# One load's issue and one cast trade places in GpSimd's order, in a fused attention and adapter kernel

## The chip, the core and the metric

The kernel runs on one core of a Trainium2 chip. The core has a matrix engine (TensorE, PE in the profile; its weight loads are PEld), a vector engine (VectorE, DVE), an activation engine (ScalarE, ACT), GpSimd (POOL) and a small engine that here only issues transfers (SyncE, SP). Data moves between the memory outside (DRAM) and the core's on-chip memory by 16 DMA engines, which serve several queues. The metric is the time of one execution on the device in microseconds (us); less is better.

## The reference

Two stages. The first is attention over 8 batch rows, 8 heads, 576 positions and head size 64, with a window of 32 positions: the plain last 32 for heads 0 to 3, and every fourth of the last 128 for heads 4 to 7. The second is a mixture of 8 low-rank adapters (rank 16), of which each token takes the best two:

```python
    mask_plain = (rel >= 0) & (rel < window)
    mask_dil = (rel >= 0) & (rel < window * dilation) & (rel % dilation == 0)
    ...
    scores = np.where(masks[None, :, :, :], scores, -1000000000.0)
    attn = np.exp(scores - max); attn = attn / sum
    x = np.matmul(attn, v)                       # [8*576, 512]
    ...
    logits = x @ w_gate                          # 8 experts, the best two by softmax
    delta[mask] += w[mask, k, None] * (x[mask] @ A[e] @ B[e])
    return x + delta
```

(The lines are condensed from the reference; inputs are float32, random with a fixed seed.)

## The kernel before

The work is cut by batch row r (0 to 7) and head group g (0: the plain heads, 1: the dilated heads, whose positions are sorted so that they too become a plain band). Each piece of work is an operation with a short name, an engine, the names that it depends on, and, if it uses PSUM, a bank. A text, PLAN, lists all 427 names in one order; the program emits them in that order, each to its own engine. So for every engine the order of its work is the order of its names in PLAN, and between engines only the waits on semaphores count, which are worked out from the dependencies. An operation whose dependencies its engine has already waited for, directly or through others, gets no wait.

The names, with row r and group g:

- L2 to L6 load a row's queries, keys and values into one of four input slots (row r into slot r mod 4), as two transfers each, one for each half of 64 partitions. Row 7 alone is loaded in eight smaller transfers: Lq7gh brings queries and keys of group g for the half h of the partitions (288 KB each in the profile), Lv7gh the values (146.2 KB each). All of these are issued by GpSimd, by `nc.gpsimd.dma_start` in line 272 (line 275 for L2 to L6).
- S0rg and S1rg are the scores on TensorE, E0rg and E1rg the exponentials on ScalarE, Vrg the product with the values on TensorE, Rrg and Nrg the reciprocal and the normalisation on VectorE (lines 381 and 384), which write the row's result X in float32.
- Brg is the cast of X to bf16 on GpSimd (line 391), Trg and Ur the transposes of it on TensorE, Crg, Cdr, Cpr their copies on ScalarE.
- Z, Y, m, s12, tt, th, top, g2 work out the logits and the gates; gzr (line 493) multiplies them on GpSimd; G transposes, gc and gn copy, D multiplies with B, and A adds the result to X (on VectorE; A73, A53, A63 in line 553 and A42, A52, A62, A72 in line 573 on GpSimd).
- Or (and Org for the last two rows) are the stores, issued by SP. Each waits for its row's A operations and, by the list `late`, for the four Lq transfers of row 7 and for Lv710 and Lv711. Each whole-row store also waits for the store before the last one to have landed.

Row 7's loads go into slot 3, which row 3 used; all eight depend on the same list, the scores and value products of row 3:

```python
        elif r == B - 1:
            free = used[r - SLOTS]
            for g in range(2):
                qk_ready[r, g] = [load(f"Lq{r}{g}{h}", r, [(h, QK_AT[h][g], QK)], free) for h in range(2)]
                v_ready[r, g] = [load(f"Lv{r}{g}{h}", r, [(h, V_AT[h][g], VB)], free) for h in range(2)]
                late.extend(qk_ready[r, g] + v_ready[r, g] * g)
```

B50, the cast of row 5's first half, depends on N50 and on the last readers of the cast's buffer, T30 and U3:

```python
        free = [f"T{r - 2}{g}", f"U{r - 2}"] if r > 1 else []
        add(f"B{tag}", "POOL", ("el", cut), lambda: [nc.gpsimd.tensor_copy(XB[r % 2][:, g, 0:cut], X[r][:, XG * g : XG * g + cut])], [nm] + free)
```

GpSimd's order around the change is, before: B40, Lq700, Lq701, B41, Lq710, gz3, B50, Lq711, Lv710, Lv711, B51, Lv700, Lv701, B60, gz4. TensorE's order in the same stretch is S150, V51, T40, T41, V50, D22, U4, G3, D21, Z04, S060, D32, Z14, S161, S160, T50, D30, S061, V60, T51, V61, U5, S171, S070, Z05, Z15, S170, S071.

Of the kernel before, what the change touches and what calls it, by code (L numbers as in the profile page):

```python
# [593 lines left out]


PLAN = """
pz0 wz warm@4 F1@1 awf btf vz00 pz2 con vz10 Lk00 Lk01 Lv00 Lv01
S000@6 vz01 vz11 tab cc1 cd3 vz20 cc0 vz21 cd2 cd0 L11 pz1 E000
F2@1 L10 cd1 S100@4 S101@6 E100 E101 L2 S001@2 E001 V00@4 R00 N00 V01@1
L3 R01 F0@0 xz0 B00 N01 B01 T00@4 vz30 L4 pz3 C00 S111@5 E111  # L600
awc S011@2 U0@0 T01@7 E011 V11@3 Cd0 Cp0 S010@1 C01 R11 vz31 E010 N11
Z00@0 Y00 m00 Z10@6 Y10 m10 S110@4 B11 s120 E110 tt0 th0 top0 V10@2
g20 gz0 T11@5 R10 N10 btc G0@1 gc0 D01@6 B10 gn0 D00@0 C11 xz1
U1@4 Cd1 Cp1 T10@5 C10 A01 A00 S121@6 E121 S120@3 S021@1 Z01@0 E021 Z11@5
Y01 m01 Y11 m11 L5 s121 S020@1 D02@0 V21@5 E120 top1 tt1 th1 g21
E020 A02 V20@0 R21 N21 R20 gz1 G1@5 gn1 F3@6 S130@6 N20 gc1 B21 E130
S031@3 D12@2 E031 S030@0 D10@5 T21@7 E030 C21 A12 S131@3 B20 V30@0 A10 E131
U2@7 T20@6 R30 N30 Cp2 B30 L6 V31@3 Cd2 C20 Z02@7 Y02 Z12@1 R31
N31 B31 T30@2 D11@6 Y12 C30 S041@4 A11 E041 S141@2 S140@6 m02 E141 S040@0
m12 s122 tt2 U3@5 Cp3 th2 E040 top2 Cd3 g22 gz2 V41@2 T31@0 E140  # L610
C31 V40@5 R41 N41 Z03@2 G2@0 Y03 gn2 Z13@1 gc2 R40 Y13 N40 B40
S051@2 D20@4 E051 A20 m13 S151@6 E151 Lq700 S050@0 S150@2 E150 m03 s123 V51@5
top3 tt3 T40@3 th3 Lq701 E050 C40 B41 g23 T41@4 C41 R51 Lq710 V50@0
N51 R50 D22@5 N50 U4@7 gz3 Cd4 Cp4 G3@6 gn3 D21@3 gc3 A22 A21
Z04@7 Y04 B50 Lq711 S060@0 D32@2 Z14@7 S161@5 m04 E060 Y14 m14 E161 s124
S160@0 A32 Lv710 T50@7 E160 D30@3 S061@5 top4 V60@0 A30 tt4 R60 C50 Lv711
O1 E061 B51 T51@3 N60 C51 V61@4 th4 g24 R61 N61 U5@7 S171@2 Cp5
Cd5 S070@0 Z05@7 E171 E070 Z15@6 Y05 S170@2 S071@4 Y15 Lv700 m05 m15 top5
Lv701 B60 gz4 E170 E071 s125 G4@0 B61 D31@6 tt5 th5 gn4 V70@1 T60@4
A31 gc4 V71@5 U6@0 C60 O0 g25 O2 gz5 G5@4 Cp6 Cd6 R70 N70  # L620
B70 T61@2 D41@0 D42@3 R71 N71 gn5 A41 C61 dx4 gc5 B71 Bx7 D40@5
Z06@2 Y06 Z16@4 Y16 A40 m06 A42 D52@3 m16 s126 dx5 top6 U7@7 Cp7
Cd7 tt6 T71@1 Cx7 C71 T70@4 D51@5 A52 th6 g26 A51 D50@0 A50 C70
gz6 Z07@2 Z17 m07 m17 s127 tt7 dy5 G6@5 gc6 O3 D61@0 th7 gn6
D62@7 A53 top7 O4 dx6 g27 D60@5 gy7 gz7 A62 dy6 O5 A61 A63
O61 G7@3 H7 gm7 gn7 gc7 D72@0 dx7 A72 D71@1 A60 D73@6 O60 A71
D70@7 O71 A70 dy7 A73 O70
"""

_INS = ["qkv", "aw", "bt", "con"]  # L630
# [60 lines left out]
```

## Time and profile before

| | us |
|---|---|
| median of 3 runs | 101.55 |
| lowest and highest of the runs | 101.32, 101.83 |
| the profiled execution's own time | 101.17 |
| its span in the profile | 99.4 |

| engine | busy us, share of the span |
|---|---|
| TensorE (matmuls) | 81.2, 82% |
| ScalarE | 71.0, 71% |
| VectorE | 62.0, 62% |
| GpSimd | 51.6, 52% |

The profile shows one execution. Times in it are counted from the start of the span. A row of the timeline gives start, duration, engine, line, operation, output and input, and in brackets how long the engine was idle before it and which engine ended that wait; "issue" is put there where the profile shows nothing that was waited for. A table of stretches gives, for each stretch of the span, the busy time and the number of instructions of each engine, then TensorE's granted clock, the share of time in which the DMA engines were busy, and what they moved in GB/s. In the queues' view q0 are the loads that GpSimd issues, q1 the stores of SP, and q8 the engines' instructions; a row gives packets, MB and the time that the packets took as a share of 16 engines' time. Landings are given as time from issue until the data has arrived.

### The profile page before, as it was taken

The page shows a single profiled execution, that of the slowest core. Times are in us where ns is not written, and L with a number is a line of the kernel's source. Part 1 is how long each engine was busy: PE and PEld are TensorE (multiplying, and loading weights), DVE is VectorE, ACT ScalarE, POOL GpSimd, SP SyncE. Part 2 cuts the span into 40 slices and gives each one's busy share as a digit, 9 for nine tenths or more (in the row PEclk, how much of TensorE's full clock was granted, in tenths as well). Part 3 has the DMA queues.
Part 4 walks back from the last instruction along what each step waited for, and adds up shares of the span by engine and source line. Part 5 has one row for each costly group of instructions (what it writes and reads, how often), then busy time and mean ns, then how long its engine had stood idle before and what let it go on. Part 6 is the DMA issues. An engine that isn't in the chain of part 4 may idle for free.

```text
span 99.4 us, 3604 instructions
## 1 busy us (share of the span) xinstructions
PE 81.2 (82%) x1587; PEld 59.8 (60%) x1587; DVE 62.0 (62%) x138; ACT 71.0 (71%) x123; POOL 51.6 (52%) x68
## 2 busy tenths in 40 slices
PE   3999969869568988999995968999999999777500
PEld 2443557458445864889674847877888878564300
DVE  5770008606469188259736665796895999979810
ACT  5294592499858964796895695979989989957400
POOL 5999402851548054404922095449458365574820
PEclk9999999999999999999999999999999999999955
DMA  1999999999999999999999999997999999839994
GB/s 19 318 206 207 207 216 228 209 209 214 207 211 217 218 216 208 209 214 205 216 208 214 218 210 210 219 197 122 198 326 408 415 412 412 352 163 415 386 421 202
DMA packets 5727, 24.50 MB, mean 247 GB/s; under 512 B 720, under 2 KB 848, under 8 KB 4944
## 3 DMA queue, kind: packets, MB, share of 16 engines
q0 software_dynamic: 3840, 14.23, 72.5%
q1 hardware_dynamic: 1728, 9.77, 24.1%
q8 instruction: 12, 0.20, 0.8%
q10 hardware_dynamic: 144, 0.28, 0.7%
q14 instruction: 3, 0.02, 0.1%
HBM read 29.07 MB, written 9.44 MB: 387 GB/s over the span
## 4 chain that ended last, share of the span: by engine, by line
PE 43%; DMA 28%; DVE 9%; ACT 6%; POOL 4%; issue 4%; POOLq 0%
PE ps L212 39%; DMA in<-in_qkv_dram 28%; DVE x L384 4%; PE ps L408 3%; ACT p L345 2%; DVE x L545 2%; POOL xb L391 2%; POOL x L553 1%; PE ps L498 1%; ACT gn L517 1%; ACT xt L418 1%; DVE rec L381 1%; POOL x L573 1%; DVE top L486 1%; ACT gc L514 1%
## 5 line engine op out<-in xcount | busy, mean ns | idle before, releaser
L391 POOL CAST xb<-x 128x1152 bf16<-128x1152 f32 (+1 forms) x16 | 18.2, 1140 | 27.6 <-DVE x L384 27.6
L345 ACT ACTIVATE p<-ps 128x960 bf16<-128x960 f32 (+1 forms) x32 | 27.6, 899 | 5.5 <-PE ps L212 5.4
L212 PE MATMUL ps<-in,p 128*64 128x130 bf16 (+1 forms) x416 | 21.3, 221 | 3.3 <-ACT p L345 3.1
L384 DVE TENSOR_TENSOR x<-ps,rec 128x1152 f32<-128x1152 f32 x16 | 21.7, 1357 | 0.5
L212 PEld LDWEIGHTS ps<-in,p 128*64 128x64 bf16 (+1 forms) x416 | 17.1, 104 | 6.7 <-ACT p L345 4.4
L545 DVE TENSOR_TENSOR x<-x,ps 128x1024 f32<-128x1024 f32 (+1 forms) x16 | 17.5, 1115 | 3.4 <-PE ps L212 3.4
L381 DVE RECIPROCAL rec<-ps 128x18 f32<-128x18 f32 x16 | 4.3, 270 | 17.4 <-PE ps L212 17.2
L493 POOL TENSOR_TENSOR gz<-zs,g 128x640 bf16<-128x640 f32 x7 | 8.9, 1275 | 11.1 <-DVE g L488 11.1
L212 PE MATMUL ps<-warm 128*128 128x512 f32 x22 | 12.7, 720 | 1.5 <-DVE warm L216 1.5
L212 PE MATMUL ps<-in 64*64 64x96 bf16 (+1 forms) x576 | 11.9, 201 | 1.5 <-issue 1.5
L212 PEld LDWEIGHTS ps<-in 64*64 64x64 bf16 x576 | 10.9, 106 | 3.7 <-issue 1.8
L272 POOL DMA_DIRECT2D in<-in_qkv_dram x22 | 11.7, 587 | 0.8 <-POOLq L674 0.8
L212 PE MATMUL ps<-aw,xt 128*128 128x136 bf16 x160 | 11.3, 223 | 0.1
L408 PE MATMUL ps<-one,xb 128*128 128x128 bf16 x128 | 9.6, 219 | 1.2 <-issue 1.2
L418 ACT COPY xt<-ps 128x1024 bf16<-128x1024 bf16 x8 | 8.1, 1011 | 3.4 <-PE ps L408 3.3
L212 PEld LDWEIGHTS ps<-aw,xt 128*128 128x128 bf16 x160 | 9.6, 98 | 0.9 <-ACT xt L418 0.4
L408 PEld LDWEIGHTS ps<-one,xb 128*128 128x128 bf16 x128 | 7.6, 97 | 2.5 <-issue 1.3
L212 PEld LDWEIGHTS ps<-warm 128*128 128x128 f32 x22 | 4.7, 232 | 6.3 <-issue 4.8
L421 ACT COPY xt<-ps 128x1024 bf16<-128x1024 bf16 x7 | 7.2, 1034 | 1.4 <-PE ps L408 1.4
L212 PE MATMUL ps<-bt,gn 128*128 128x256 bf16 (+1 forms) x48 | 6.8, 263 | 1.5 <-ACT gn L517 0.8
L212 PE MATMUL ps<-bt,gc 128*128 128x256 bf16 (+1 forms) x48 | 6.6, 255 | 1.5 <-ACT gc L514 1.5
L466 ACT COPY zs<-ps 128x408 f32<-128x408 f32 (+1 forms) x14 | 5.9, 459 | 2.0 <-PE ps L212 2.0
(54 smaller groups left out, 98.0 us busy)
## 6 DMA issues: line engine op xcount, KB each, us to landing
in<-in_qkv_dram POOLq DMA_DIRECT2D x10, 868.5 KB, 23.1
out_dram<-x SPq DMA_DIRECT2D x6, 1152.0 KB, 5.8
in<-in_qkv_dram POOLq DMA_DIRECT2D x10, 288.0 KB, 8.1
out_dram<-x SPq DMA_DIRECT2D x4, 576.0 KB, 3.0
in<-in_qkv_dram POOLq DMA_DIRECT2D x10, 146.2 KB, 8.1
in<-in_qkv_dram POOLq DMA_DIRECT2D x2, 434.2 KB, 13.5
awf<-in_aw_dram ACTq DMA_DIRECT2D x1, 272.0 KB, 3.7
btf<-in_bt_dram SPq DMA_DIRECT2D x1, 256.0 KB, 3.5
```

The lines of the kernel that those rows point to most:

```text
L212: return nc.tensor.matmul(o, lhsT=lhsT, rhs=rhs, start=start, stop=stop, skip_group_check=True)
L272: nc.gpsimd.dma_start(out=IN[r % SLOTS][half(a), at : at + n], in_=qkv[r, a, :, at - 2 * VB * a : at - 2 * VB * a + n],) if n < ROW else n ...
L345: return [nc.scalar.activation(p[:, :, :].rearrange("p h (s c) -> p h s c", c=PER)[:, :, b0 : b0 + nb, 0:SEG], PS[:, k.at : k.at + 2, 0 : ...
L381: rc = add(f"R{tag}", "DVE", ("el", 60), lambda: [nc.vector.reciprocal(rec[:, :].rearrange("p (b i) -> p b i", b=3), PS[:, k.at : k.at + 3 ...
L384: nm = add(f"N{tag}", "DVE", ("el", XG), lambda: [nc.vector.tensor_tensor(X[r][:, XG * g : XG * g + XG].rearrange("p (b i n) -> p b i n", ...
L391: add(f"B{tag}", "POOL", ("el", cut), lambda: [nc.gpsimd.tensor_copy(XB[r % 2][:, g, 0:cut], X[r][:, XG * g : XG * g + cut])], [nm] + free)
L408: nc.tensor.transpose(tp[j][:, 128 * u : 128 * u + 128], xb[:, g, 256 * u + 128 * j : 256 * u + 128 * j + 128], ident())
L418: return [nc.scalar.copy(xt[:, 0:2, 0:S].rearrange("p j (c i) -> p j c i", c=C)[:, :, :, 0:128], tp.rearrange("p j (i c) -> p j c i", c=C))]
L421: return [nc.scalar.copy(xt[:, 2:4, 0:512], tp)]
L466: zc.append(add(f"Y{st}{r}", "ACT", ("el", len(us) * ZW), lambda us=us, k=k: [nc.scalar.copy(zs[:, us[0] : us[-1] + 1].rearrange("p u n -> ...
L493: return [en.tensor_tensor(GZ[i][:, us[0] : us[0] + n, :].rearrange("p u (e r) -> p u e r", e=E), zv()[:, us[0] : us[0] + n, 0:ER].rearran ...
L545: return [nc.vector.tensor_tensor(v, v, PS[:, k.at : k.at + nk].rearrange("p b n -> p (b n)"), ALU.add)]
```

## The change

In PLAN, and so in GpSimd's order, Lq711 now stands ahead of B50 where it stood right behind it. All other names keep their places; the text of PLAN is only broken into lines afresh. The order on the other engines stays the same, and no operation is added or taken away. The diff cut to its core:

```diff
 ...
-Z04@7 Y04 B50 Lq711 S060@0 D32@2 Z14@7 S161@5 m04 E060 Y14 m14 E161 s124
+gn3 D21@3 gc3 A22 A21 Z04@7 Y04 Lq711 B50 S060@0 D32@2 Z14@7 S161@5 m04
 ...
```

GpSimd's order afterwards is: B40, Lq700, Lq701, B41, Lq710, gz3, Lq711, B50, Lv710, Lv711, B51, Lv700, Lv701, B60, gz4.

More of the change, by code (lines that the diff above doesn't have):

```diff
@@ L596 @@
 PLAN = """
[L597 to L612, printed above, removed]
@@ L613 @@
-top3 tt3 T40@3 th3 Lq701 E050 C40 B41 g23 T41@4 C41 R51 Lq710 V50@0
-N51 R50 D22@5 N50 U4@7 gz3 Cd4 Cp4 G3@6 gn3 D21@3 gc3 A22 A21
-Z04@7 Y04 B50 Lq711 S060@0 D32@2 Z14@7 S161@5 m04 E060 Y14 m14 E161 s124
[L616 to L627, printed above, removed]
+pz0 wz warm@4 F1@1 awf btf vz00 pz2 con vz10 Lk00 Lk01 Lv00 Lv01 S000@6
+vz01 vz11 tab cc1 cd3 vz20 cc0 vz21 cd2 cd0 L11 pz1 E000 F2@1 L10 cd1
@@ new lines @@
+S100@4 S101@6 E100 E101 L2 S001@2 E001 V00@4 R00 N00 V01@1 L3 R01 F0@0
+xz0 B00 N01 B01 T00@4 vz30 L4 pz3 C00 S111@5 E111 awc S011@2 U0@0 T01@7
+E011 V11@3 Cd0 Cp0 S010@1 C01 R11 vz31 E010 N11 Z00@0 Y00 m00 Z10@6 Y10
+m10 S110@4 B11 s120 E110 tt0 th0 top0 V10@2 g20 gz0 T11@5 R10 N10 btc
+G0@1 gc0 D01@6 B10 gn0 D00@0 C11 xz1 U1@4 Cd1 Cp1 T10@5 C10 A01 A00
+S121@6 E121 S120@3 S021@1 Z01@0 E021 Z11@5 Y01 m01 Y11 m11 L5 s121
+S020@1 D02@0 V21@5 E120 top1 tt1 th1 g21 E020 A02 V20@0 R21 N21 R20 gz1
+G1@5 gn1 F3@6 S130@6 N20 gc1 B21 E130 S031@3 D12@2 E031 S030@0 D10@5
@@ new lines @@
+T21@7 E030 C21 A12 S131@3 B20 V30@0 A10 E131 U2@7 T20@6 R30 N30 Cp2 B30
+L6 V31@3 Cd2 C20 Z02@7 Y02 Z12@1 R31 N31 B31 T30@2 D11@6 Y12 C30 S041@4
+A11 E041 S141@2 S140@6 m02 E141 S040@0 m12 s122 tt2 U3@5 Cp3 th2 E040
+top2 Cd3 g22 gz2 V41@2 T31@0 E140 C31 V40@5 R41 N41 Z03@2 G2@0 Y03 gn2
+Z13@1 gc2 R40 Y13 N40 B40 S051@2 D20@4 E051 A20 m13 S151@6 E151 Lq700
+S050@0 S150@2 E150 m03 s123 V51@5 top3 tt3 T40@3 th3 Lq701 E050 C40 B41
+g23 T41@4 C41 R51 Lq710 V50@0 N51 R50 D22@5 N50 U4@7 gz3 Cd4 Cp4 G3@6
@@ new lines @@
+gn3 D21@3 gc3 A22 A21 Z04@7 Y04 Lq711 B50 S060@0 D32@2 Z14@7 S161@5 m04
+E060 Y14 m14 E161 s124 S160@0 A32 Lv710 T50@7 E160 D30@3 S061@5 top4
+V60@0 A30 tt4 R60 C50 Lv711 O1 E061 B51 T51@3 N60 C51 V61@4 th4 g24 R61
+N61 U5@7 S171@2 Cp5 Cd5 S070@0 Z05@7 E171 E070 Z15@6 Y05 S170@2 S071@4
+Y15 Lv700 m05 m15 top5 Lv701 B60 gz4 E170 E071 s125 G4@0 B61 D31@6 tt5
+th5 gn4 V70@1 T60@4 A31 gc4 V71@5 U6@0 C60 O0 g25 O2 gz5 G5@4 Cp6 Cd6
+R70 N70 B70 T61@2 D41@0 D42@3 R71 N71 gn5 A41 C61 dx4 gc5 B71 Bx7 D40@5
@@ L628 @@
+Z06@2 Y06 Z16@4 Y16 A40 m06 A42 D52@3 m16 s126 dx5 top6 U7@7 Cp7 Cd7 tt6
+T71@1 Cx7 C71 T70@4 D51@5 A52 th6 g26 A51 D50@0 A50 C70 gz6 Z07@2 Z17
+m07 m17 s127 tt7 dy5 G6@5 gc6 O3 D61@0 th7 gn6 D62@7 A53 top7 O4 dx6 g27
+D60@5 gy7 gz7 A62 dy6 O5 A61 A63 O61 G7@3 H7 gm7 gn7 gc7 D72@0 dx7 A72
+D71@1 A60 D73@6 O60 A71 D70@7 O71 A70 dy7 A73 O70
 """
```

## The prediction

> **What bounds the kernel now.** I read the page's engine lines and its chain first, then the stretches of the chain on the timeline.
>
> ```profile
> PE 81.2 (82%) x1587; PEld 59.8 (60%) x1587; DVE 62.0 (62%) x138; ACT 71.0 (71%) x123; POOL 51.6 (52%) x68
> PE 43%; DMA 28%; DVE 9%; ACT 6%; POOL 4%; issue 4%; POOLq 0%
> q8 instruction: 12, 0.20, 0.8%
> in<-in_qkv_dram POOLq DMA_DIRECT2D x10, 288.0 KB, 8.1
> 20.58 27.80 DMA in<-in_qkv_dram
> ...
> 78.97 1.29 PE ps L212 x26
> ```
>
> The chain of waits is led by TensorE. In order of time (the last two rows) it is the load queue until 48.4 us and TensorE from about there to 80.26 us, where V71 ends, so the edited stretch (63 to 70 us) lies where TensorE sets the pace, and GpSimd is half idle. The third line is a queue that no line of the kernel issues: 12 transfers, 0.20 MB, 16 KB each. They are the program's own instructions. The fourth has the size of row 7's Lq transfers.
>
> The second view is GpSimd's timeline around the edit.
>
> ```profile
> 60.40 0.53 POOL L272 DMA_DIRECT2D in<-in_qkv_dram  x1
> 62.05 1.27 POOL L493 TENSOR_TENSOR gz<-zs,g 128x640 bf16<-128x640 f32 x1 [1.11 <-DVE g L488]
> 65.86 1.14 POOL L391 CAST xb<-x 128x1152 bf16<-128x1152 f32 x1 [2.55 <-DVE x L384]
> 66.95 1.62 POOL L272 DMA_DIRECT2D in<-in_qkv_dram  x3
> 68.52 1.20 POOL L391 CAST xb<-x 128x1152 bf16<-128x1152 f32 x1
> 69.61 1.07 POOL L272 DMA_DIRECT2D in<-in_qkv_dram  x2
> ```
>
> These are Lq710, gz3, B50, then Lq711 with Lv710 and Lv711, B51, then Lv700 with Lv701. GpSimd stands idle for 2.55 us ahead of B50, waiting for VectorE's N50; the moved issue sat behind that wait and now goes in front of it.
>
> The third view is TensorE's weight loads where they stopped for no reason on another engine, and with it the table of stretches cut at these stops.
>
> ```profile
> 53.61 0.32 PEld L408 LDWEIGHTS ps<-one,xb 128*128 128x128 bf16 x5 [1.30 <-issue]
> 60.12 0.11 PEld L212 LDWEIGHTS ps<-in 64*64 64x64 bf16 x2 [1.43 <-issue]
> 66.63 0.22 PEld L212 LDWEIGHTS ps<-in 64*64 64x64 bf16 x14 [0.34 <-issue]
> core 0: us, PE busy (x) PEld busy (x) DVE busy (x) ACT busy (x) POOL busy (x), PEclk, DMA share, GB/s
> 53.60:60.10 6.50, 5.21 (x127) 4.19 (x126) 4.02 (x11) 4.46 (x7) 2.97 (x4) 1.00 1.06 213
> 60.10:66.60 6.50, 6.27 (x126) 5.31 (x127) 4.82 (x9) 5.53 (x10) 2.84 (x4) 1.00 1.05 213
> 66.60:71.20 4.60, 4.58 (x128) 3.69 (x128) 3.48 (x11) 4.07 (x6) 4.07 (x7) 1.00 0.87 151
> 71.20:75.94 4.74, 4.72 (x128) 4.01 (x129) 3.33 (x5) 4.07 (x9) 2.75 (x3) 1.00 1.06 330
> ```
>
> Three stops, two of them in the middle of one score tile, and between one and the next 126 to 127 pairs of weight load and matmul: about 254 instructions, a 16 KB block. I read them as TensorE having run out of instructions. By the same count the next two blocks begin at 71.20 and at 75.94, and there it did not stop.
>
> The fourth view, the queues in narrow stretches, says when a block was fetched. These are 57.45 to 57.50, 64.00 to 64.05, 67.7 to 67.8 and 72.98 to 73.05 (the share is of 16 engines in the stretch, so 160.0% of 0.05 us is 1.28 us for the transfer).
>
> ```profile
> q8 instruction: 1, 0.02, 160.0%
> q8 instruction: 1, 0.02, 156.1%
> q8 instruction: 1, 0.02, 55.9%
> q8 instruction: 1, 0.02, 115.4%
> ```
>
> Durations: 1.28, 1.25, 0.89 and 1.29 us. The first two end at 58.75 and 65.27, and TensorE goes on at 60.12 and 66.63: 1.37 us later, both times. And if a block is asked for when the one before it begins, the transfer started 3.86 us after the asking (53.61 to 57.47) and 3.90 us (60.12 to 64.02) with the load queue full, but 1.12 us (66.63 to 67.75) in the third stretch. That stretch is the one with 151 instead of 213 GB/s. The hole, 62 GB/s over 4.60 us or 0.285 MB, is nearly one Lq transfer (288.0 KB, 0.295 MB): the one that the edit brings forward.
>
> **The change part by part.** The cast and the issue trade places in GpSimd's order; nothing is added or removed. Lq711 has no wait of its own left (Lq700 waited for the same list), so it can go when gz3 ends, at 62.05 + 1.27 = 63.32, and its 0.53 us (Lq710's row) end at 63.85, 2.0 us before B50 can start. B50 therefore loses nothing: cover 2.55, cost 0.53; were the idle time gone, B50 would be 0.53 us late. Behind B50 the two remaining issues end 0.53 us earlier, and B51 starts at 67.99 instead of 68.52. TensorE does not use that:
>
> ```profile
> 68.56 0.45 PEld L408 LDWEIGHTS ps<-one,xb 128*128 128x128 bf16 x8
> 71.21 0.49 PEld L408 LDWEIGHTS ps<-one,xb 128*128 128x128 bf16 x8
> 73.24 0.14 PEld L212 LDWEIGHTS ps<-con,one 64*64 64x64 bf16 x4 [0.16 <-issue]
> ```
>
> T51 reads B51 at 71.21, 1.5 us after the cast ended. So on GpSimd the change is worth zero.
>
> On the load queue, the landings of Lq710, Lq711 and the last pair of late loads, from the loads' view in the stretches 60 to 61, 66.9 to 67.4 and 67.9 to 68.5:
>
> ```profile
> DMA to landing us min/median/max: 8.3/8.3/8.3
> DMA to landing us min/median/max: 4.0/4.0/4.0
> DMA to landing us min/median/max: 4.1/4.2/4.3
> ```
>
> Lq710 lands at 68.7, Lq711 at 70.95, and Lv711, the third of three issues that take 1.62 us from 66.95 on, at 68.03 + 4.3 = 72.3. Issued at 63.3, Lq711 follows Lq710 directly: 0.295 MB at 213 GB/s is 1.38 us, so it lands at about 70.1, 0.85 us earlier. Its first reader S171 starts at 73.24 (the row above), so that is worth zero as well; the late loads are done 0.5 to 0.8 us earlier, which only lets the stores begin.
>
> What is left is what the filled hole does to the instruction block that TensorE needs at 71.20. No run shows a fetch behind exactly this queue, so I bound its lag. Lower end: 1.12 us as now. Upper end: 3.9 us, the full queue of the earlier stretches. To do no harm it must start by 71.20 - 1.37 - 1.28 = 68.55, a lag of 1.92. In my reading the fetch waits for the descriptors that already stand on its engine; before, those were the rest of Lq710, afterwards that rest and Lq711: 1.12 + 1.38 = 2.50 us. I take this value, since it is made of the nearest row and of the one transfer that moves. The fetch then starts at 69.13, takes 1.28 (the load queue is full again, Lv710 being there from 66.95 on), and TensorE goes on at 69.13 + 1.28 + 1.37 = 71.78. **Cost: 0.58 us.** With a lag of 1.12 it would be zero; with 3.9, 70.53 + 2.65 = 73.18, that is 2.0 us; with a transfer of 0.89 at a lag of 2.5, 0.2 us.
>
> The stop falls at T51. From there to 80.26 TensorE has next to no slack (4.72 busy of 4.74 in the last row of the table), and VectorE's and ScalarE's work in that stretch comes from it, so I pass all of it on. Sum against the profiled execution (101.17 us, of which 99.4 are the span): 0 - 0 + 0.58 = 101.75. That execution stands 0.38 under the median of the runs, 101.55; on the median the sum gives 102.13, which I round to 102.1.
>
> Two rules of the Trainium skill speak against this. DMA: Bandwidth & Descriptors, in Queues, rings and completion order, says that each DMA engine goes round its queues and changes over after a packet. By that rule the fetch would wait for Lq710's packet alone and the sum would be zero; the lags of 3.86 and 3.90, alike within 0.04 us, look more like a fixed depth of queue, but one lag of 1.12 doesn't exclude it. Runtime: NRT & Kernel Launch, in Instruction fetch mechanics, has blocks of 256 instructions fetched while the one before runs, mostly hidden. The block size agrees with the 126 to 127 pairs here; the hiding doesn't, at 1.43 us of stop.
>
> **The rivals.** First, *the fetch keeps its lag*: one queue gets its turn after the packet in work, whatever stands behind it. For it: the lag of 1.12 ended about when Lq710 did (landing at 68.7, with the last bytes some time before). Against it: 3.9 us twice. Even with the longer transfer, 67.75 + 1.28 + 1.37 = 70.40 is in time. Time: 101.55.
>
> Second, *two stops or one long one*. If the lag is 3.9, 2.0 us: 103.5. Or the first stop shifts the next asking from 71.20 to 71.78, while the stores come earlier, and the fetch falls behind a store. Lags behind stores are long: the block asked for at 75.94 was fetched at 79.37 (stretch 79.35 to 79.40), 3.4 us.
>
> ```profile
> q8 instruction: 1, 0.02, 116.8%
> 72.37 8.69 SPq L586 DMA_DIRECT2D out_dram<-x  x4
> ```
>
> 71.78 + 3.4 + 1.29 + 1.37 = 77.8 against 75.94 + 0.58 = 76.5, 1.3 us more, 103.4 in all. It decides at O1's issue: now at 72.37, 1.2 us after the asking at 71.20, whose fetch (72.98 to 73.05) lagged by 1.8; afterwards 71.5 to 72.3 against 71.78.
>
> Third, on the other side, *the stores carry the gain to the end*: faster by up to the 0.8 us of the landings, 100.75. O1 to O3 do come earlier. But further on the stores wait for compute:
>
> ```profile
> SPq L139 <- DMA out_dram<-x: 9.5, 3, 4.4
> SPq L139 <- POOL x L553: 5.5, 3, 4.2
> SPq L590 <- DVE x L545: 0.5, 1, 0.5
> 84.00:85.00 1.00, 1.00 (x19) 0.89 (x17) 0.97 (x8) 1.00 (x6) 0.24 (x1) 1.00 0.55 210
> 88.00:89.00 1.00, 0.52 (x10) 0.34 (x6) 0.70 (x7) 0.44 (x1) 0.74 (x1) 1.00 0.16 65
> 93.89 1.26 POOL L553 TENSOR_TENSOR x<-x,btf 128x512 f32<-128x512 f32 x1 [0.23 <-ACT btf L551]
> ```
>
> SP waits 4.2 us for GpSimd's A53, and the DMA engines are down to 0.55 and 0.16 of their time at 84 and 88 us. Stores that come earlier only widen these holes; the last one still waits for A73, which ends at 95.15. The rival needs both holes closed.
>
> That the change doesn't do what it says, Lq711 still waiting for something at 63.3, would leave everything at 101.55; it is counted with the first rival.
>
> **How the numbers follow.** About 0.5% (0.51 us) is what a measurement of this kernel can tell from no change; the three runs lie 0.51 us apart. One stop of 0.2 to 0.65 us: chance 0.47, of which 0.34 go beyond 0.5% and 0.13 stay within. The first rival: 0.26, within. The second: 0.18, slower. The third: 0.09, faster. Together faster 0.09, same 0.39, slower 0.52. The likeliest case has a range of 101.75 to 102.2. The whole range begins at 101.2, the first rival less the 0.35 us by which runs differ from their median, and goes to 103.3, nearly up to the two-stop cases at 103.4 and 103.5; left out are these cases' upper part and the third rival.
>
> **What would show it.** After: an issue row of 0.53 us at about 63.3 and B50 still at 65.9; no hole in the load queue between 66.6 and 71.2 (213 instead of 151 GB/s); the q8 transfer of 67.7 now at about 69.1; a stop named "issue" of about 0.6 us on TensorE near 71.2, and V71's end moved from 80.26 to about 80.8. The forecast is wrong if the q8 transfer stays at 67.7 (then no change), if it comes after 70 (then over a microsecond), if a second stop stands at 76, or if B50 is late, which would mean that the issue was not covered by the idle time.

## The result

The changed kernel takes 1.0063 of the time of the kernel before, with a 95% interval of 1.0040 to 1.0087: slower by 0.64 us on 101.55. The forecast was 102.1, 0.56% slower, with 0.52 of the chance on slower. The ratio compares the fast runs alone and holds for them alone: over all 22 runs of each kernel the medians lie the other way round, 101.51 after and 101.61 before, with five runs of before and two of after above 102.3 us.

GpSimd's timeline of the changed kernel, around the edit:

```profile
61.09 1.27 POOL L493 TENSOR_TENSOR gz<-zs,g 128x640 bf16<-128x640 f32 x1 [0.73 <-DVE g L488]
62.32 0.58 POOL L272 DMA_DIRECT2D in<-in_qkv_dram  x1
64.92 1.14 POOL L391 CAST xb<-x 128x1152 bf16<-128x1152 f32 x1 [2.02 <-DVE x L384]
66.00 1.03 POOL L272 DMA_DIRECT2D in<-in_qkv_dram  x2
67.01 1.18 POOL L391 CAST xb<-x 128x1152 bf16<-128x1152 f32 x1
```

Lq711 is issued at 62.32, right behind gz3, and B50 still waits 2.02 us for VectorE's N50 after it. On GpSimd the issue was free. TensorE's weight loads where they stopped, the stretches between the stops, and the queue of instructions in the stretch 68.95 to 69.05:

```profile
53.03 0.32 PEld L408 LDWEIGHTS ps<-one,xb 128*128 128x128 bf16 x5 [0.50 <-issue]
59.17 0.10 PEld L212 LDWEIGHTS ps<-in 64*64 64x64 bf16 x2 [0.75 <-issue]
71.43 0.10 PEld L212 LDWEIGHTS ps<-in,p 128*128 128x128 bf16 x1 [1.45 <-issue]
...
52.90:59.15 6.25, 5.24 (x127) 4.20 (x126) 4.13 (x8) 4.82 (x8) 2.73 (x5) 1.00 1.06 214
59.15:65.40 6.25, 6.23 (x126) 5.32 (x127) 4.91 (x13) 5.38 (x10) 3.50 (x5) 1.00 1.05 214
65.40:69.90 4.50, 4.50 (x131) 3.60 (x127) 3.51 (x11) 4.14 (x7) 3.75 (x6) 1.00 1.06 205
69.90:71.40 1.50, 0.20 (x4) 0.08 (x2) 0.00 (x0) 0.55 (x1) 0.00 (x0) 1.00 1.02 187
...
q8 instruction: 1, 0.02, 55.8%
```

A new stop of 1.45 us stands at T51 (its first row is the last weight load of V60), again 126 to 127 pairs behind the one before. In the last stretch TensorE ran 0.20 of 1.50 us. The hole in the load queue is filled: the DMA engines, at 0.87 between 66.60 and 71.20 us before, are at 1.06 and 1.02 in the last two stretches. The block was fetched at about 69.0, where the kernel before fetched it at 67.75.

The stop is longer than the whole loss. In this execution the two earlier stops, which the change cannot touch, were shorter (0.50 and 0.75 us against 1.30 and 1.43 in the first profile of before; what sets their length is open), so TensorE reached the block early and waited the longer. That is why the spans, 99.6 and 99.4, differ little, and why V71 ends at 80.54, only 0.28 later:

```profile
79.25 1.29 PE ps L212 x26
```

### The profile page after: what moved, and what is told of

It is laid out like the page before. It is cut to its first block, busy times and chain, and to the rows that moved or that the text cites. A ratio compares the mean times of both kernels' runs of the same rounds, so it can differ in the third digit from the quotient of the medians.

```text
span 99.6 us, 3604 instructions
## 1 busy us (share of the span) xinstructions
PE 81.5 (82%) x1587; PEld 59.8 (60%) x1587; DVE 61.5 (62%) x138; ACT 71.2 (71%) x123; POOL 51.7 (52%) x68
## 4 chain that ended last, share of the span: by engine, by line
PE 43%; DMA 25%; ACT 11%; DVE 8%; issue 4%; POOL 4%; POOLq 0%
PE ps L212 39%; DMA in<-in_qkv_dram 25%; ACT p L345 4%; PE ps L408 3%; DVE x L384 3%; DVE x L545 2%; POOL x L553 1%; ACT in L262 1%; POOL xb L391 1%; ACT gn L517 1%; PE ps L498 1%; ACT xt L418 1%; ACT xt L421 1%; POOL x L573 1%; ACT zs L466 1%
```

## The experiments

The theory, called "block" below: the bytes of Lq711 stand on the DMA engines ahead of the 16 KB of instructions for T51's block, and TensorE runs out. The rivals: something at T51 itself is waited for ("place"), or it matters that row 7's data comes early ("data"). Measured times are given as shares of the time of the kernel before, with the 95% interval. Those of the kernels called shift40, dummy and gate6 rest on six runs each, from 102.1 us up, a range that single runs of the kernel before reach too (up to 103.9 us), so their size is unsure; I go by their stops and fetches.

**Does the stop go with the place in the work or with the count of instructions?** Forty small matmuls were put behind the warm-up.

```diff
+    add("sm", "PE", ..., lambda: [mm(bank(k_sm)[0:64, 0:64], WARM[:, 0:64], WARM[:, 0:64], True, True)
+        for _ in range(40)][:0], ["warm"], k_sm)
-... warm@4 F1@1 awf ...
+... warm@4 F1@1 sm@2 awf ...
```

> The changed kernel with 40 small extra matmuls on TensorE right behind the warm-up (their result is not used), so that every 16 KB block of instructions begins 40 pairs earlier in the work. Theory 'block' (TensorE stops at a block whose fetch stands behind Lq711's descriptors): the stop at 70 to 71.6 us is no longer at T51 but 40 pairs earlier, inside S061, as an 'issue' stop of 1 to 2.3 us that ends between 71.0 and 71.7; the earlier stops move by 40 pairs too; time 1.003 to 1.015 of the kernel before. Rival 'place' (T51 itself waits for something, B51 or a bank): the stop stays at T51, whatever the count.

Measured: 1.0231 (1.0159 to 1.0304). Weight loads on the timeline of this kernel:

```profile
52.71 0.18 PEld L212 LDWEIGHTS ps<-in 64*64 64x64 bf16 x9 [1.29 <-issue]
64.80 0.17 PEld L212 LDWEIGHTS ps<-in,p 128*128 128x128 bf16 x3 [0.57 <-issue]
70.98 0.23 PEld L212 LDWEIGHTS ps<-in 64*64 64x64 bf16 x15 [0.46 <-issue]
```

The stop at T51 is gone, and one stands in the middle of S061's 20 matmuls, as the count says. It ends at 70.98; at 0.46 us it is shorter than expected, since TensorE came later. Place falls. The loss of 2.3% is larger than expected, with stops at other places (64.80, and one more near 81). Some of it is there long before the edited stretch: a group of score matmuls that starts at 48.42 in the kernel before starts at 49.32 here. How much is the extra matmuls themselves is not separated.

**Is it the filled queue or the early data?** In one kernel the old order stays, and an extra load of the same size, which nobody reads, is issued ahead of B50. In another Lq711 comes early, but Lq710 late in its place.

```diff
 dummy (on the kernel before)
+            add("Ldum", "POOL", ..., lambda: [nc.gpsimd.dma_start(out=IN[0][half(1), 2 * VB : 2 * VB + QK],
+                in_=qkv[B - 1, 1, :, 0:QK])], used[4])
-Z04@7 Y04 B50 Lq711
+Z04@7 Y04 Ldum B50 Lq711
 swap (on the kernel before): Lq710 and Lq711 trade places
-... C41 R51 Lq710 V50@0 ... Z04@7 Y04 B50 Lq711
+... C41 R51 Lq711 V50@0 ... Z04@7 Y04 B50 Lq710
```

> The kernel before, in its old order (B50 ahead of Lq711), with one extra load of Lq711's size and source issued between gz3 and B50 into a slot that nothing reads any more: the load queue is filled as by the change, but none of row 7's loads comes earlier. Theory 'block': a stop at T51 as in the changed kernel, ending at about 71.6, the q8 transfer of that block at about 69.0 instead of 67.7; time 1.003 to 1.012. Rival 'data' (what costs is that row 7's data and with it the stores come earlier): no stop at T51, time 0.997 to 1.003, since the late loads land up to 0.6 us later and the stores have holes to lose that in.

> The kernel before with Lq710 and Lq711 in each other's places: Lq711 is now issued early (ahead of B50, at about 60.4), Lq710 late (behind B50, at about 67). The load queue holds as much at every moment as before. Theory 'block': no stop at T51, the q8 transfer at about 67.7 as before, time 0.996 to 1.004. Rival 'data' (an early Lq711 in itself costs time): a stop or a loss as in the changed kernel, 1.004 to 1.01.

Measured: dummy 1.0175 (1.0100 to 1.0249), swap 0.9995 (0.9947 to 1.0043). Of the kernel with the extra load, GpSimd's issue of it, the stop on the weight loads, and the instruction queue from 69.3 to 69.4:

```profile
62.36 0.58 POOL L578 DMA_DIRECT2D in<-in_qkv_dram  x1
71.73 0.10 PEld L212 LDWEIGHTS ps<-in,p 128*128 128x128 bf16 x1 [1.45 <-issue]
q8 instruction: 1, 0.02, 60.1%
```

Of the kernel with the two loads swapped, the stops and the queue from 67.8 to 67.9:

```profile
70.07 0.10 PEld L212 LDWEIGHTS ps<-in,p 128*128 128x128 bf16 x1 [0.45 <-issue]
75.08 0.27 PEld L212 LDWEIGHTS ps<-in 64*64 64x64 bf16 x19 [0.20 <-issue]
q8 instruction: 1, 0.02, 55.9%
```

The useless load makes the same stop, of the same 1.45 us; the early Lq711 without a fuller queue makes one of 0.45 us (TensorE was there at 69.6 already) and no loss. So data falls, and the queue is shown. The time with the extra load is beyond the 1.012 expected at most; what the rest comes from is not shown.

**Does the stop grow with the bytes?** Half as much ahead of B50 (Lv710 in place of Lq711), and one and a half times as much (Lq711 and Lv710).

```diff
 half_early (on the kernel before)
-Z04@7 Y04 B50 Lq711 ... A32 Lv710 T50@7
+Z04@7 Y04 Lv710 B50 Lq711 ... A32 T50@7
 two_early (on the changed kernel)
-Z04@7 Y04 Lq711 B50 ... A32 Lv710 T50@7
+Z04@7 Y04 Lq711 Lv710 B50 ... A32 T50@7
```

> The kernel before with Lv710 (half the bytes of Lq711) issued between gz3 and B50 in place of Lq711, which stays behind B50. Theory 'block': the fetch stands behind 0.7 us of additional data and not 1.4, so that it comes at about 68.4 and TensorE can go on at about 70.7; a stop of 0 to 0.6 us, time 1.000 to 1.005. If any entry in the queue is enough, whatever its size: stop to 71.5, 1.005 to 1.01.

> The changed kernel with Lv710 too ahead of B50 (gz3, Lq711, Lv710, B50, Lv711): 0.7 us more in the queue. If the fetch waits for everything that was issued ahead of it: q8 transfer at about 69.9, stop until about 72.2, time 1.010 to 1.018. If the wait is limited to some 3.5 to 3.9 us, as the lags of the full queue in all profiles so far suggest: q8 transfer by 69.5, stop until 71.6 to 71.8 as in the changed kernel, time 1.004 to 1.010.

Measured: half_early 1.0010 (0.9968 to 1.0051), two_early 1.0031 (0.9975 to 1.0087). With half, the stop and the queue from 68.55 to 68.65:

```profile
70.80 0.10 PEld L212 LDWEIGHTS ps<-in,p 128*128 128x128 bf16 x1 [0.63 <-issue]
q8 instruction: 1, 0.02, 60.9%
```

The fetch moves with the bytes put ahead of it: 67.8 with none more (swap), 68.6 with half, 69.0 with all of Lq711, 69.35 with the extra load, although TensorE came to the block before, at which I take it to ask for this one, at nearly the same time in all four (65.0 to 65.7). TensorE goes on at 70.07, 70.80, 71.43 and 71.73, which is 2.2 to 2.45 us after the fetch began each time. That is the size of the effect in four steps. With one and a half the interval reaches from no loss to 0.9%: it excludes the 1.010 to 1.018 of a queue without limit and says no more. Its profile does not help: after an earlier stop of 2.22 us and 3.4 us at half the clock (more on this below) TensorE asked for the block at 67.94, some 2.5 us later than in the changed kernel's profile.

**What limits the queue: descriptors or something else?** Rows 2 to 6 in twice as many runs of half the size, and row 7's Lq transfers in three runs each, both on the changed kernel.

```diff
 runs6
-RUNS, PAD = 3, 16
+RUNS, PAD = 6, 16
 q7three (row 7 is laid out in DRAM with gaps to match)
-out=IN[...][half(a), at : at + n], in_=qkv[r, a, :, ...]
+out=o.rearrange("p (j n) -> p j n", j=3), in_=qkv[B - 1, a, :, c : c + QKP].rearrange("p (j n) -> p j n", j=3)[:, :, 0 : QK // 3]
```

> The changed kernel with rows 2 to 6 loaded in 6 runs of 2316 bytes per partition in place of 3 of 4632; same bytes. Fixed number of descriptors: the lag of the blocks asked for at 53.6 and 60.1 us halves to about 1.9 us and the stops near 52 and 58 us shrink from 1.3 and 1.4 us to under 0.4; the stop at T51 stays and still ends at about 71.6, since its fetch stands behind Lq710 and Lq711, so that the time is 1.000 to 1.008 of the kernel before. Fixed amount of bytes: stops near 52 and 58 as before, time 1.004 to 1.01.

> The changed kernel with each Lq transfer of row 7 cut into three runs of 1536 bytes per partition (768 elements) by gaps in DRAM; same bytes, same order, three times the descriptors. Theory 'block' with a queue that holds a fixed number of descriptors (3.9 us of the 4632-byte ones, about 11): 11 descriptors of 1536 bytes are 1.3 us, so the fetch comes at about 67 to 68 us, no stop at T51, time 0.993 to 1.002. If the queue holds a fixed amount of bytes, or everything that was issued: stop as in the changed kernel, 1.004 to 1.01.

Measured: runs6 1.0124 (1.0082 to 1.0167), q7three 1.0090 (1.0050 to 1.0131). Of the first, a stop and the queue from 58.1 to 58.2; of the second, the stop at T51 and the queue from 68.55 to 68.65:

```profile
54.54 0.53 PEld L408 LDWEIGHTS ps<-one,xb 128*128 128x128 bf16 x5 [1.78 <-issue]
q8 instruction: 1, 0.02, 62.2%
```

```profile
70.97 0.10 PEld L215 LDWEIGHTS ps<-in,p 128*128 128x128 bf16 x1 [1.27 <-issue]
q8 instruction: 1, 0.02, 55.8%
```

The lag in the full queue is 3.6 us (54.54 to 58.17) with descriptors of half the size, as it was 3.9 before, and the stop at T51 is there with row 7's descriptors of a third. By these two a fixed number of descriptors, which I had thought likely, falls. Less clear is the next block of runs6: it was fetched 2.35 us after TensorE asked at 60.84; but at the same block two_early, with whole descriptors, has 2.0 us. Against what I expected, runs6 has no stop at T51, where TensorE comes only at 72.2, and its time is above both ranges; in this execution the stop at T51 is therefore not what made it slow. Whether the limit is one of bytes or of time is open.

**The mechanism turned round.** If early issues cost, a late one should gain: L6 was made to wait for T31, which ends at about 54, just after TensorE asks for a block. And a wider hole was tried, with Lq710 behind B50 too.

```diff
 gate6 (on the kernel before)
-used.get(r - SLOTS, [])
+used.get(r - SLOTS, []) + (["T31"] if r == 6 else [])
-... Cp2 B30 L6 V31@3 ... T31@0 E140
+... Cp2 B30 V31@3 ... T31@0 L6 E140
 hole2 (on the kernel before)
-... R51 Lq710 V50@0 ... Y04 B50 Lq711
+... R51 V50@0 ... Y04 B50 Lq710 Lq711
```

> The kernel before with row 6's load L6 issued only when T31 is done (about 54 us, not 47): the same mechanism turned round. When TensorE asks for a block at 53.6, only the rest of L5 stands in the queue, and not L6. Theory 'block': that q8 transfer starts at 55 to 56 in place of 57.5, the stop near 58.8 (1.4 us) falls under 0.4, L6 still lands at 65 to 65.5, and as nothing is ahead of the block of 66.6 and T51, TensorE keeps part of it: time 0.985 to 0.998. If the lag comes from the load on the DMA engines and not from what was issued before: stop unchanged, 0.998 to 1.005.

> The kernel before with Lq710 too behind B50 (gz3, B50, Lq710, Lq711, Lv710, Lv711): the hole in the load queue becomes two transfers wide and opens at 65.5 to 66.9. Theory 'block': the block for T51 comes at 66.5 to 67, no stop there even when TensorE is early (a gain of up to 0.4 us); but the next block, asked for at 70 to 71, stands behind the loads that moved back and comes up to 3.5 us after the asking, so that TensorE stops near 75 for 0.3 to 1.2 us. Time 0.998 to 1.010. If only the block for T51 counted: 0.993 to 1.000.

Measured: gate6 1.0184 (1.0129 to 1.0240), hole2 0.9975 (0.9905 to 1.0046). Of gate6, the queue from 54.5 to 54.6 and the main waits of the weight loads:

```profile
q8 instruction: 1, 0.02, 82.6%
53.51 0.32 PEld L408 LDWEIGHTS ps<-one,xb 128*128 128x128 bf16 x5 [0.23 <-issue]
57.49 0.11 PEld L212 LDWEIGHTS ps<-con,one 64*64 64x64 bf16 x4 [0.90 <-DMA in<-in_qkv_dram]
66.97 0.11 PEld L212 LDWEIGHTS ps<-one 64*64 64x64 bf16 x4 [1.68 <-DMA in<-in_qkv_dram]
73.31 0.10 PEld L212 LDWEIGHTS ps<-in,p 128*128 128x128 bf16 x1 [1.51 <-issue]
```

The block asked for at 53.5 was fetched 1.0 us later in place of 3.9, and the stop near 59 is gone: the queue is again what decides. But the time got worse. I had assumed that L6 would still land by 65.5; S060 waited 1.68 us for it until 66.97. The stop at T51 fits the queue that is now late, though I did not test that by itself. Of hole2, T51, a later wait and the queue from 66.6 to 66.7:

```profile
70.41 0.46 PEld L408 LDWEIGHTS ps<-one,xb 128*128 128x128 bf16 x8 [0.19 <-issue]
74.99 0.47 PEld L212 LDWEIGHTS ps<-aw,xt 128*128 128x128 bf16 x8 [1.06 <-DVE x L384]
q8 instruction: 1, 0.02, 77.9%
```

The fetch came at 66.65 as expected. The stop for instructions that I expected near 75 did not come; TensorE waited there for VectorE, 1.06 us by the profile. The time can't be told from that of before. No version is shown to beat both kernels.

**Second profiles of the two kernels.**

> The kernel before once more, for a second profile. Theory 'block': where the stops near 53 and 59 us are short and TensorE asks for the block at about 65.3, that block comes at 67.7 to 68.0 and TensorE goes on at T51 by 70.1 at the latest, with a stop of 0 to 0.5 us; where the early stops are long as in the first profile, no stop at T51. In neither case does it go on later than 71.2.

> The changed kernel once more, for a second profile. Theory 'block': q8 transfer at 68.3 to 69.8 and TensorE going on at T51 between 71.2 and 72.0, whatever the stops before it were; the stop there is 1.2 to 1.6 us after short early stops and under 0.7 after long ones.

One execution each, 100.83 before and 102.18 after. Of before, T51, the next stop and the queue from 67.7 to 67.8; of after, the first stop, T51 and the queue from 68.95 to 69.05:

```profile
70.31 0.46 PEld L408 LDWEIGHTS ps<-one,xb 128*128 128x128 bf16 x8
75.72 0.27 PEld L212 LDWEIGHTS ps<-in 64*64 64x64 bf16 x19 [0.69 <-issue]
q8 instruction: 1, 0.02, 55.9%
```

```profile
54.47 0.32 PEld L408 LDWEIGHTS ps<-one,xb 128*128 128x128 bf16 x5 [1.95 <-issue]
72.26 0.49 PEld L408 LDWEIGHTS ps<-one,xb 128*128 128x128 bf16 x8
q8 instruction: 1, 0.02, 67.1%
```

Before, with short early stops, fetches at 67.75 again and does not stop at T51; but it then stops for 0.69 us one block on, which the changed kernel's first profile does not. After, with a long early stop, TensorE comes to T51 at 72.26, past the 71.2 to 72.0 that I expected, and the block has long been there: no stop at T51.

The second profile of before and the first of after are the nearest pair: both have short early stops, and TensorE asks for T51's block at 65.64 and 65.42. It begins that block at 70.17 before and 71.43 after, the next at 75.72 and 76.14, and V71 ends at 79.95 and 80.54:

```profile
78.66 1.29 PE ps L212 x26
```

Of 1.26 us, 0.59 are left at V71 and 0.60 in the spans (99.05 and 99.65 us). So where TensorE is early, a part of the stop is given back one block later; where it is late, as in the second profile of after, there is no stop to pay for. One pair is not an average: that 0.6 us agrees with the 0.64 us of the runs does not show how the runs divide into such cases.

What makes the early stops 0.5 us in one execution and 1.3 to 2.2 in another is open. One thing goes with the longest: in the three profiles with 1.78, 1.95 and 2.22 us (runs6, the second of after, two_early) TensorE's granted clock is 0.5 for 3.4 us, starting at 54.3 to 55.3, and in no other profile is it below 1.00 between 45 and 90 us. That adds to TensorE's late arrival at T51 in these three.

## Why the prediction was right

*GpSimd, zero.* Right: issue at 62.32 in the idle time, B50 not late, B51 1.5 us ahead in this execution, of which 0.5 are the issue, and T51 doesn't wait for it.

*The fetch, a lag of 2.50 us.* The mechanism was right, that the fetch waits for bytes issued ahead of it, and so was the time of the fetch: 69.0 against 69.13. The lag itself was 3.6 us (65.42 to 68.98), since the queue's end does not move with TensorE; when TensorE asks earlier, it waits longer. In the kernel before (two profiles) and in swap the fetch came at 67.74, 67.76 and 67.82, asked for at 66.63, 65.64 and 65.03. The kernels dummy, swap and half_early show that it is the bytes in front. That it is all of them, as the sum had it, is doubtful (see the landings below).

*The stop, 0.58 us.* TensorE went on at 71.43 against 71.78; the difference is mostly the transfer, 0.89 us (55.8% of 0.1 us on 16 engines) and not 1.28. The term that was mis-sized is the other end of the stop: I took 71.20, from the one profile that I had, for the time at which TensorE arrives, and in the four profiles of the two kernels it lies between 70.0 and 72.2. The stop was therefore 1.45 in one execution and 0 in another. That the sum came out near 0.64 all the same is partly luck: I passed all of the stop on and knew nothing of what is given back at 76. Behind that, passing it on was right: from V71's end to the end of the span it is 19.1 us in all four profiles of the two kernels.

*The first rival, a turn after the packet in work,* falls: with it the fetch would have come no later than at 67.75. The rule of the Trainium skill, DMA: Bandwidth & Descriptors, Queues, rings and completion order, that an engine changes over after a packet, does not hold here in the form that the prediction gave it, with Lq710 as the packet; what an engine took as one packet no trace shows, so the rule itself is not decided. What the Trainium skill says in Runtime: NRT & Kernel Launch, Instruction fetch mechanics, that crossing into a new block is mostly hidden, held for T51's block in both profiles of before, where the load queue had a hole (no stop), and often not where the queue was full: most of the profiles stop for 0.5 to 2.2 us near 53 or 59.

*The second rival, a second stop behind the stores,* did not show in the changed kernel's two profiles. A stop at that block, of 0.69 us, is in the second profile of before.

*The third rival, earlier stores,* and the step under it, late loads 0.5 to 0.8 us earlier, fall. Landings of Lq711 and of the pair Lv710 and Lv711 (from 62.3 to 62.8 and from 66.5 to 67 in the loads' view), the stores' row, SP's wait for A53 and the holes between the stores, all of the changed kernel:

```profile
DMA to landing us min/median/max: 9.1/9.1/9.1
DMA to landing us min/median/max: 5.8/5.9/6.1
72.64 16.79 SPq L586 DMA_DIRECT2D out_dram<-x  x6
SPq L139 <- POOL x L553: 5.5, 3, 4.2
84.00:85.00 1.00, 1.00 (x17) 0.78 (x16) 0.97 (x7) 1.00 (x6) 0.00 (x0) 1.00 0.55 219
88.00:89.00 1.00, 0.80 (x14) 0.63 (x11) 0.73 (x7) 0.16 (x1) 1.00 (x1) 1.00 0.16 65
```

Issued at 62.32, Lq711 landed at 71.4, later than the 70.95 of before and not at 70.1, and O1 went at 72.64 against 72.37. Nothing on TensorE waited for either. In the trace's list of packets, 254 of the 256 pieces (4608 bytes each) of row 7's Lq loads start by 69.09, and the last two at 69.86 and 70.29, right behind the fetch, which ran from 68.98 to 69.88. The list does not name the engine, but it looks as if the fetch went ahead of the end of Lq711 on its engine: that would explain the late landing, and would mean that the fetch does not wait for everything issued before it. The argument that the stores' gain would be lost in the later holes needed no gain to lose: the holes are as they were.

## What to carry to other kernels

An issue that costs its engine nothing can still cost time through what it puts ahead of others on the DMA engines, and one of these others is the program itself. Where the busiest engine stops in the middle of a tile for "issue", count its instructions between the stops; if the count is a constant, look when the instruction queue moved its 16 KB and what was in front of it. A hole in the load queue is not always waste: before filling it, ask whose transfer went through it.

## What the runs showed of the hardware

With the load queue full, the instruction block that TensorE asks for near 53 us was fetched 3.5 to 4.0 us later in twelve of the thirteen profiles, with descriptors of 4632 and of 2316 bytes alike; the one after it, 2.0 to 4.3 us later. Where the queue was running out (the first profile of before at 66.63, gate6 at 53.51, hole2 at 65.60) it was 1.0 to 1.1 us. The time of asking is an assumption, the start of the block before. The transfer took 0.9 to 1.3 us, and where TensorE had stopped for it, it went on 1.2 to 1.7 us after the transfer's end. With the queue full that makes about 6 to 6.5 us for a block of 126 to 127 pairs of weight load and matmul (6.51 and 6.51 between the stops of the first profile of before, 6.14 between those of after), and TensorE, which here needs 4.5 to 6.3 us for one, can run faster than its instructions come.
